# Output products one step later, two element-wise sets interleaved on VectorE, all output copies on ScalarE

## Chip, cores, metric

One core of one Trainium2 chip. The metric is the device time of one execution in microseconds, here 1134.75 us as the median of three runs (1134.71 to 1135.37).

## What is computed

The reference is a linear attention followed by a two-layer network. For each of 8 batches and 8 heads (576 tokens, head size 64), queries and keys go through a feature map of 128 features, `exp` of plus and minus the projection less its largest magnitude. Sums over keys give `kv` and `z`, and each query's output is a quotient. The heads are put together to x, 4608 tokens by 512, and then

```python
h = x @ w_in            # 512 -> 2048
g = h - np.tanh(h)
return (g @ w_out)      # 2048 -> 512
```

## The kernel before

**First part** (up to some 329 us): attention, 32 units of two heads; x goes transposed to DRAM (`xs`). Meanwhile the weights of the network are decoded into f32 tiles (`dec_*`), and some are split. Each unsplit weight tile has a home (`HOME`, `w_home`): a `tl` slot of a lasting pool, or a pool that is closed when group 1 begins. `second` closes that pool and opens another, `rp`, with the weight sums `th`, and with slots `tp` and `xs`.

**Second part** (from line 552): the network. Tokens are cut into 9 groups of 512 (four tiles of 128). The hidden width of 2048 is cut into 16 blocks f of 128, and a step handles one group g and one pair of blocks j (f = 2j and 2j+1): 72 steps s, group by group. Each f32 operand is kept as a high part in fp32r and a low remainder, and each product is made of three matmuls, high with high, high with low, low with high.

In groups 0 and 1 (steps 0 to 15) a step is *plain*: `plain` makes 12 matmuls of 512 columns for each block (4 chunks of the contraction, 3 each), into one PSUM tile for each block. The tiles alternate between the pairs y, x and w, v. From group 2 on (`FOLD`, steps 16 to 71) a step is *folded*: seven products of quarter size (`product`, six matmuls of 256 columns each, 42 in all) of sums and differences of weight and token quarters, and VectorE adds them up to the same two blocks, in Y (first token half) and X (second token half). W holds products 1 and 6, V 5 and 7, Y 2 and 3, X's first half 4. The adds are u3 (line 884), K (885), the Y add (891) and the two X adds (892, 893). K's first part is a ScalarE copy of product 1.

Each step gives two *sets* (`Set`): in a plain step one for each block with all four token tiles, in a folded step one for tiles 0 and 1 and one for tiles 2 and 3, with both blocks. A set is a 128x512 piece of h on which `h - tanh(h)` is made with care near zero. Its instructions are, by name: `y_` (square, ScalarE), `s1_`, `s2_` (squares with an offset, ScalarE), `th_` (tanh), `mk_` (mask of large values, ScalarE), `d1`, `d2`, `d3` (polynomial, VectorE, lines 610, 613, 616), `d4` (h minus tanh, 619), `d5` (select by the mask, 622), `gh_` (high part, ScalarE, 626), `gl_` (low part, GpSimd, 630). The tiles `y`, `s1`, `th` and `mk` have one buffer for both sets, `s2`, `gh` and `gl` two. `d1`, `d2`, `d5` read two SBUF tiles; `d3`, `d4` and the five adds read PSUM.

`q` multiplies a set's high and low parts by the output weights `wo[g, f]` into one PSUM tile per token tile (four buffers): for one token tile and a folded set six matmuls of 512 columns. After the last pair of blocks of a group the four tiles are copied out of PSUM (`finish`) and stored by DMA. `wo_fetch` loads a step's two output weights (512 KB each) on SP's queue into four buffers in turn.

All instructions of the second part are issued in an order written out by hand, the loop over s at the end of the function. Each engine takes its own in that order. `one` and `two` are the last step's two sets. Other work is hung into the loop by `job(s, place, ...)` and comes out at `do(s, place)`: weight splits of group 0 (`LOWS`), loads, the weight sums for the folded products (`t_load`/`t_new`, `t_add`, `t_hi`, `t_lo`; one j a step), the last four units' denominators (`den_mul`, `x_store`), and each next group's token operands: for group 1 plain ones, from group 2 on seven sums and differences (`x_sum` on GpSimd, `x_hi` on ScalarE, `x_lo` on GpSimd). Their places are the slots of `x_slot`. GpSimd's jobs at place `p1` stand behind a tiny copy (`mark`, line 903) that reads a VectorE result.

Of the kernel before, what the change touches and what calls it, by code (L numbers as in the profile page):

```python
# [19 lines left out]
P = 128  # L20
# [12 lines left out]
def tile_linear_attention_moe(  # L33
# [57 lines left out]
    HOME = {("i", f): f for f in range(NI, NF)} | {("o", f): f - NO for f in range(NO, NO + NI)}  # L91
# [42 lines left out]
    slots = [*range(12), 0, 1, 2, 3, 4, 5, 6, 7, 12]  # L134

    def x_slot(nm):
        k = slots.pop(0)
        if not slots:
            slots.extend((8, 9, 10, 11, 0, 1, 2, 3, 4, 5, 6, 7, 12))
        return (tp[0] if k == 12 else xp[k // 4]).tile([P, 2, DM], F32R, tag="tp" if k == 12 else f"xc{k}", name=f"xc{nm}")  # L140

    with ExitStack() as c1:
# [301 lines left out]
        def period(i):  # L444
# [42 lines left out]
            if last:  # L487
                for j in range(NCT):
                    x0.append(x_slot(f"0_{j}"))
                    nc.scalar.copy(x0[j][:, 0, :], xt[0][:, j, :])  # L490
                    nc.vector.tensor_tensor(x0[j][:, 1, :], xt[0][:, j, :], f32(x0[j][:, 0, :]), ALU.subtract)
# [60 lines left out]
    with ExitStack() as c2, tc.manual_schedule():  # L552
# [12 lines left out]
        def second():  # L565
            late.close()
            pool = c2.enter_context(tc.tile_pool(name="rp", bufs=1, reuse_waits="tile", side="right"))
            th.extend(pool.tile([P, DM], F32R, name=f"th{j}") for j in range(NP))
            tp.append(pool)
            xp.append(pool)  # L570
# [8 lines left out]
        class Set:  # L579
            def __init__(self, s, half, h, fs, tiles):  # L580
                self.g, self.j = steps[s]
                self.s, self.h, self.fs, self.tiles = s, h, fs, tiles
                self.nm = f"{s}_{half}"
                self.left = list(tiles)
# [52 lines left out]
        ends = []  # L637
        mark = gp.tile([P, 1], F32, name="gate")

        def q(v, most=4):  # L640
            if v is None:
                return
            g = v.g
            for t in v.left[:most]:
                v.left.remove(t)
                if (g, t) not in po:
                    po[g, t] = [ps_o.tile([P, DM], F32, tag="o", name=f"po{g}_{t}"), False]
                o, begun = po[g, t]
                n = v.tiles.index(t)
                cuts = [slice((a * len(v.tiles) + n) * P, (a * len(v.tiles) + n + 1) * P) for a in range(len(v.fs))]  # L650
                last = v.fs[-1] == NF - 1
                for f, cut in zip(v.fs, cuts):
                    for k in range(2):
                        nc.tensor.matmul(o, v.gh[:, cut], wo[g, f][:, k, :], start=not begun, stop=False)  # L654
                        begun = True
                for f, cut in zip(v.fs, cuts):
                    nc.tensor.matmul(o, v.gl[:, cut], wo[g, f][:, 0, :], start=False, stop=last and f == v.fs[-1])  # L657
                po[g, t][1] = True
                if last:
                    ends.append((g, t))  # L660

        def finish(g, t):
            pool, tag = (gp, "o") if t < 2 else (tp[0], "xs")
            o = pool.tile([P, DM], F32, tag=tag, name=f"o{g}_{t}", bufs=2)
            if t % 2:
                nc.scalar.copy(o, po[g, t][0])
            else:
                nc.vector.tensor_copy(o, po[g, t][0])
            nc.sync.dma_start(out[(g * GT + t) * P : (g * GT + t + 1) * P, :], o)
# [55 lines left out]
        def t_new(j):  # L725
            pool, tag = (xp[0], "xc3") if j % 2 and j < NP - 1 else (tp[0], "tp")
# [34 lines left out]

        xsum = {}
# [8 lines left out]
        def x_new(g, n):  # L771
            xc.setdefault(g, {})[n] = x_slot(f"{g}_{n}")
# [28 lines left out]
        def job(s, where, fn, *args):  # L801
            jobs.setdefault((s, where), []).append((fn, args))
# [6 lines left out]
        LOWS = ["i8 i9 o8", "i10 i11 o9", "o4 o5 i12", "o6 o7", "i13 o10 o11", "i14 i15 o12", "o13 o14 o15"]  # L809
# [7 lines left out]
        for j, s in enumerate((9, 10, 11, 12, 13, 14, 15, 19)):  # L817
            job(s - 1, "d1", t_load if 2 * j < NI else t_new, j)
            job(s, "d1", t_add, j)
            job(s, "a1", t_hi, j)  # L820
            job(s + 1, "v0", t_lo, j)
# [3 lines left out]
        for k, s in enumerate((0, 1, 2, 3)):  # L825
            job(s, "p1", den_mul, units[NU - 4 + k], nc.gpsimd)
            job(s, "p1", x_store, units[NU - 4 + k])
        for g in range(1, NG):
            z = NP * (g - 1)

            def fresh(c, g=g):
                if c == 0:
                    xr[g] = x_raw(g)
                x_load(g, xr[g], slice(c, c + 2))

            job(z, "d1", fresh, 0)
            job(z + 1, "d", fresh, 2)
            if g < FOLD:
                for c, n in enumerate((4, 5, 6, 7) if g == 1 else (2, 3, 5, 6)):
                    job(z + n, "a", x_plain, g, c)  # L840
                    job(z + n, "p1", x_plain_lo, g, c)
                continue
            for n, where, fn, k in (
                (1, "a", x_hi, 1), (1, "p1", x_lo, 1),
                (2, "p0", x_sum, 5), (2, "a", x_hi, 2), (2, "p1", x_lo, 2),
                (3, "p0", x_sum, 6), (3, "a", x_hi, 5), (3, "p1", x_lo, 5),
                (4, "p0", x_sum, 3), (4, "a", x_hi, 6), (4, "p1", x_lo, 6),
                (5, "p0", x_sum, 7), (5, "a", x_hi, 3), (5, "p1", x_lo, 3),
                (6, "a", x_hi, 7), (6, "p1", x_lo, 7),
                (7, "a", x_hi, 4), (7, "p1", x_lo, 4),  # L850
            ):
                job(z + n, where, fn, g, k)

        for s in range(NS + 1):
            one, two = sets.get((s - 1, 0)), sets.get((s - 1, 1))
            g, j = steps[s] if s < NS else (None, None)
            do(s, "d")
            fold = g is not None and g >= FOLD
            if g is not None:
                Y, X = (ps_x.tile([P, GN], F32, tag=t, name=f"y{s}" if a == 0 else f"x{s}") for a, t in enumerate("yx" if fold or s % 2 else "wv"))  # L860
                if g:
                    wo_fetch(g, j)
            if fold:
                W, V = (ps_x.tile([P, GN], F32, tag=t, name=f"{t}{s}") for t in "wv")
                r = {1: W[:, lo_], 6: W[:, hi_], 2: Y[:, lo_], 3: Y[:, hi_], 4: X[:, lo_], 5: V[:, lo_], 7: V[:, hi_]}
                K = gp.tile([P, 3, HN], F32, tag="k", name=f"k{s}")
                for n in (1, 6, 5, 7):
# [4 lines left out]
            if g is not None:  # L872
                cur = [Set(s, a, h, (2 * j, 2 * j + 1) if fold else (2 * j + a,), (2 * a, 2 * a + 1) if fold else (0, 1, 2, 3)) for a, h in enumerate((Y, X))]
            run(two, "d3", "d4", "d5")
            do(s, "v0")
            do(s, "d1")
            run(two, "gh_")
            run(one, "gl_")
            run(two, "gl_")
            do(s, "p0")  # L880
            if fold:
                u3 = K[:, 2, :]
                both = u3.unsqueeze(1).broadcast_to([P, 2, HN])
                tt(u3, r[6], K[:, 0, :], ALU.add)
                tt(K[:, 1:3, :], V.rearrange("p (a n) -> p a n", a=2), both, ALU.add)  # L885
                for n in (3, 2):
                    product(r[n], g, j, n)
                if s < NS - 1:
                    q(one, 1)
                product(X[:, lo_], g, j, 4)  # L890
# [3 lines left out]
            elif g is not None:  # L894
                plain(X, g, 2 * j + 1)
            q(one)
            q(two)
            do(s, "a")
            if g is not None:
                new, nxt = cur  # L900
                run(new, "y_", "s1_", "s2_", "th_", "mk_", "d1", "d2")
                if (s, "p1") in jobs:
                    nc.gpsimd.tensor_copy(mark, new.s1[:, 0:1])
                do(s, "p1")
                run(new, "d3", "d4", "d5")
                run(nxt, "y_", "s1_", "s2_")
                run(new, "gh_")
                do(s, "v1")
                run(nxt, "th_", "mk_", "d1", "d2")
            do(s, "p2")  # L910
            do(s, "v")
            do(s, "a1")
            while ends:
                finish(*ends.pop(0))
            if g is not None:
                sets[s, 0], sets[s, 1] = cur
# [55 lines left out]
```

## Time and profile before

| | |
|---|---|
| median of three runs | 1134.75 us |
| profiled execution: time, span | 1136.19 us, 1134.4 us |
| granted TensorE clock, mean | 0.998 |
| busy TensorE, VectorE, ScalarE, GpSimd | 98%, 85%, 76%, 46% |
| first matmul of step 0, first of step 16 | 328.84 us, 501.38 us |

The span runs from the first to the last instruction; the profiled execution's time has 1.79 us around it. In the rows of a timeline the first figure is the start, the second the duration, both in us from the span's start; then engine, line, operation, what is written and read, how many; in brackets the idle time before it and what ended it. PE is TensorE, PEld its weight loads, DVE VectorE, ACT ScalarE, POOL GpSimd, SP the queue of the DMAs. In the rows by stretch the columns are the stretch, its length, busy us and count for PE, PEld, DVE, ACT and POOL, then granted clock, busy share of the DMA engines, GB/s. A row of one line of code gives count, then shortest, median and longest duration in ns.

### The profile page before, as it was taken

To read this page: it belongs to the slowest core of one execution; us is meant where nothing else is said; L and a number is where in the kernel's file an instruction comes from. 1 tells how busy PE (TensorE), PEld (TensorE's weight loads), DVE (VectorE), ACT (ScalarE), POOL (GpSimd) and SP (SyncE) were. 2 spreads that over 40 slices of the span, in tenths; PEclk is the share of its full clock that TensorE was granted. 3 is DMA by queue.
4 is the path that set the end of the run, shared out by engine and by line. 5 is a ranking of instruction groups with operands and counts; after the bars stand their busy time and mean duration, and the time that the engine had idled before them with its cause. 6 is when DMAs were issued, how large, how long until landed. Compare 5 with 4: busy or idle time off the path is not lost. (4 is left out here: it accounts for less than half of the span.)

```text
span 1134.4 us, 22407 instructions
## 1 busy us (share of the span) xinstructions
PE 1113.2 (98%) x8010; PEld 894.6 (79%) x8010; DVE 964.5 (85%) x1478; ACT 860.4 (76%) x1716; POOL 525.5 (46%) x508
## 2 busy tenths in 40 slices
PE   9999999999999999999899999999999999999997
PEld 6666666666667888888788888888888888888885
DVE  6888889888879879998888888888888888888886
ACT  5888888888888877677677777777777776877765
POOL 4665665565534434443443543543543543443231
PEclk9999999999999999999999999999999999999999
DMA  5576766667624246324225325234333323422432
GB/s 162 181 242 220 237 216 211 237 219 246 204 92 153 97 155 198 112 93 151 92 82 179 106 81 185 77 111 152 108 113 127 133 96 115 161 76 95 136 105 75
DMA packets 76048, 165.41 MB, mean 146 GB/s; under 512 B 16672, under 2 KB 31392, under 8 KB 75936
## 3 DMA queue, kind: packets, MB, share of 16 engines
q1 hardware_dynamic: 75776, 163.90, 43.2%
q8 instruction: 64, 1.05, 0.4%
q14 instruction: 48, 0.39, 0.1%
q10 hardware_dynamic: 160, 0.07, 0.0%
HBM read 134.28 MB, written 29.51 MB: 144 GB/s over the span
## 5 line engine op out<-in xcount | busy, mean ns | idle before, releaser
L630 POOL TENSOR_TENSOR gl<-s,gh 128x512 fp32r<-128x512 f32 x143 | 216.9, 1517 | 325.2 <-ACT gh L626 188.5
L654 PE MATMUL po<-wo,gh 128*128 128x512 f32 x1152 | 326.8, 396 | 5.5 <-ACT mk L607 3.4
L654 PEld LDWEIGHTS po<-wo,gh 128*128 128x128 f32 x1152 | 209.3, 189 | 49.1 <-ACT mk L607 4.6
L657 PE MATMUL po<-wo,gl 128*128 128x512 f32 x576 | 197.7, 406 | 5.4 <-POOL gl L630 5.1
L626 ACT CAST gh<-s 128x512 fp32r<-128x512 f32 x144 | 89.5, 621 | 109.1 <-DVE s L622 99.1
L657 PEld LDWEIGHTS po<-wo,gl 128*128 128x128 f32 x576 | 104.8, 189 | 47.7 <-POOL gl L630 26.0
L610 DVE SCALAR_TENSOR_TENSOR s<-s,y 128x512 f32<-128x512 f32 x144 | 99.4, 690 | 47.8 <-ACT s L595 47.8
L255 DVE TENSOR_REDUCE m<-pp 128x4 f32<-128x512 f32 (+3 forms) x98 | 92.0, 940 | 40.9 <-PE pp L245 37.4
L314 POOL TENSOR_TENSOR ss<-ss,kp 128x512 f32<-128x512 f32 x96 | 122.9, 1280 | 8.0 <-ACT kp L299 3.0
L622 DVE COPY_PREDICATED s<-mk,th 128x512 f32<-128x512 uint32 x144 | 111.1, 771 | 15.2 <-ACT s L595 0.5
L595 ACT ACTIVATE s<-y,bias_t 128x512 f32<-128x512 f32 x144 | 104.3, 724 | 20.0 <-DVE s L616 11.1
L299 ACT ACTIVATE kp<-t 128x256 f32<-128x256 f32 (+2 forms) x256 | 108.8, 484 | 7.8 <-DVE t L262 7.0
L613 DVE SCALAR_TENSOR_TENSOR s<-s,s 128x512 f32<-128x512 f32 x144 | 99.7, 693 | 15.0
L607 ACT ACTIVATE mk<-y,bias_t 128x512 f32<-128x512 f32 x144 | 102.6, 712 | 0.0
L599 ACT ACTIVATE s<-y,bias_t 128x512 f32<-128x512 f32 x144 | 102.1, 709 | 0.0
L245 PEld LDWEIGHTS pp<-wph,qk 64*128 64x128 f32 x1152 | 72.1, 187 | 33.3 <-PE po L350 13.1
L262 DVE TENSOR_TENSOR t<-pp,m 128x512 f32<-128x512 f32 (+3 forms) x98 | 92.0, 941 | 3.3
L245 PE MATMUL pp<-wph,qk 64*128 64x128 f32 x1152 | 90.3, 289 | 1.2 <-PE pk L319 0.8
L591 ACT ACTIVATE y<-y 128x512 f32<-128x512 f32 x72 | 43.0, 597 | 63.9 <-DVE y L891 57.8
L713 PE MATMUL y<-xc,hl 128*128 128x256 f32 x672 | 89.3, 282 | 1.7 <-DVE th L619 1.7
L713 PEld LDWEIGHTS y<-xc,hl 128*128 128x128 f32 x672 | 84.1, 189 | 2.0 <-issue 1.6
L713 PEld LDWEIGHTS w<-xc,hl 128*128 128x128 f32 x560 | 78.0, 188 | 5.1
(396 smaller groups left out, 2242.7 us busy)
## 6 DMA issues: line engine op xcount, KB each, us to landing
wo<-wod SPq DMA_DIRECT2D x128, 512.0 KB
qk<-in_qkT SPq DMA_DIRECT2D x31, 576.0 KB
v<-in_v SPq DMA_DIRECT2D x32, 320.0 KB
rb<-rr SPq DMA_DIRECT2D x64, 144.0 KB
xs<-rb SPq DMA_DIRECT2D x32, 288.0 KB
out<-o SPq DMA_DIRECT2D x36, 256.0 KB
rawi<-in_moe_w_in SPq DMA_DIRECT2D x16, 512.0 KB
rawo<-in_moe_w_out SPq DMA_DIRECT2D x16, 512.0 KB
```

Source lines behind the costliest of these rows:

```text
L245: nc.tensor.matmul(heads[e][:, o * F : (o + 1) * F], u.qk[hs, j * P : (j + 1) * P], wph[hs, :], start=True, stop=True)
L299: nc.scalar.activation(o, x, AF.Exp, scale=1.0 - 2.0 * s)
L314: nc.gpsimd.tensor_tensor(u.ss, u.ss, u.kp[:, :, j], ALU.add)
L595: nc.scalar.activation(self.s1, self.y, AF.Square, bias=bias_t[:, 0:1])
L599: nc.scalar.activation(self.gs, self.y, AF.Square, bias=bias_t[:, 1:2])
L607: nc.scalar.activation(self.mk, self.y, AF.Relu, bias=bias_t[:, 2:3])
L613: stt(self.s1, self.gs, PC2, self.s1, ALU.add, ALU.mult)
L622: nc.vector.copy_predicated(self.gs, self.mk.bitcast(U32), self.th)
L630: (nc.vector if self.s == NS - 1 and self.tiles[0] else nc.gpsimd).tensor_tensor(self.gl, self.gs, f32(self.gh), ALU.subtract)
L654: nc.tensor.matmul(o, v.gh[:, cut], wo[g, f][:, k, :], start=not begun, stop=False)
L657: nc.tensor.matmul(o, v.gl[:, cut], wo[g, f][:, 0, :], start=False, stop=last and f == v.fs[-1])
L713: nc.tensor.matmul(o, w[:, k], x[:, a, m], start=(i == 0), stop=(i == 5))
```

## The change

- Outputs a step later. The loop knows a third set, `old`, the second set of two steps ago. A step's output products are now `q(old)` in the middle of the step's hidden products and `q(one)` behind them; `q(two)` in the same step is gone. Folded: products 1, 6, 5, 7; `q(old)`; 3, 2, 4; `q(one)`. In a folded set, `q` runs the high matmuls of both tiles first and then the low ones. The loop has one more turn at its end.
- VectorE's order in a folded step: `d3`, `d4` of `two`; the five adds; `d5` of `two`; then `d1` to `d5` of the new first set, `d1`, `d2` of the second. `mk_` of a folded second set moves to the next step on ScalarE, and `gh_`, `gl_` of `two` come behind the new set's squares.
- All four output copies of a group go to ScalarE; the tiles lie in token slots instead of own ones.
- The weight sums move to steps 8 to 15 (before: 9 to 15, and j = 7 in step 19). The homes of unsplit output weights change (`HOME`), so that o8 to o15 outlast the closed pool, and the split of o15 moves to step 7.
- The last units' denominators go to steps 1 to 4 instead of 0 to 3, group 1's token operands one step earlier with their low parts where they were. From group 3 on all GpSimd token work is at place `p0`, ahead of the low parts, with no `mark`.

```diff
-        def q(v, most=4):
+        def q(v):
...
+            if nt == 2:
+                for part in (high, low):
+                    for n in range(nt):
+                        part(n)
             else:
-                nc.vector.tensor_copy(o, po[g, t][0])
+                for n in range(nt):
+                    high(n)
+                    low(n)
+
+        def finish(n):
+            while ends and ends[0][1] < n:
+                store(*ends.pop(0))
+
+        def store(g, t):
+            if t % 2 == 0:
+                out_t[g, t // 2] = x_slot(g + 2, f"o{g}_{t}", 2 + t // 2, F32)
+            o = out_t[g, t // 2][:, t % 2, :]
+            nc.scalar.copy(o, po[g, t])
...
-        for j, s in enumerate((9, 10, 11, 12, 13, 14, 15, 19)):
-            job(s - 1, "d1", t_load if 2 * j < NI else t_new, j)
-            job(s, "d1", t_add, j)
+        for j in range(NP):
+            s = NP + j
+            job(s - 1 if j else s, "d1" if j else "d", t_load if 2 * j < NI else t_new, j)
+            job(s, "d1" if j else "v", t_add, j)
...
-        for s in range(NS + 1):
-            one, two = sets.get((s - 1, 0)), sets.get((s - 1, 1))
+        for s in range(NS + 2):
+            one, two, old = sets.get((s - 1, 0)), sets.get((s - 1, 1)), sets.get((s - 2, 1))
...
-            run(two, "d3", "d4", "d5")
+            q(old)
+            finish(2)
+            do(s, "a")
+            if not plain_two:
+                run(two, "mk_")
+            finish(4)
+            run(two, "d3", "d4")
+            if not fold:
+                run(two, "d5")
             do(s, "v0")
             do(s, "d1")
-            run(two, "gh_")
-            run(one, "gl_")
-            run(two, "gl_")
             do(s, "p0")
             if fold:
-                u3 = K[:, 2, :]
-                both = u3.unsqueeze(1).broadcast_to([P, 2, HN])
                 tt(u3, r[6], K[:, 0, :], ALU.add)
-                tt(K[:, 1:3, :], V.rearrange("p (a n) -> p a n", a=2), both, ALU.add)
-                for n in (3, 2):
+                tt(K[:, 1:3, :], V.rearrange("p (a n) -> p a n", a=2), u3.unsqueeze(1).broadcast_to([P, 2, HN]), ALU.add)
+                for n in (3, 2, 4):
                     product(r[n], g, j, n)
-                if s < NS - 1:
-                    q(one, 1)
-                product(X[:, lo_], g, j, 4)
+            elif g is not None:
+                plain(X, g, 2 * j + 1)
+            q(one)
+            if fold:
                 tt(Y, Y, K[:, 0:2, :].rearrange("p a n -> p (a n)"), ALU.add)
                 tt(X[:, hi_], r[5], u3, ALU.add)
                 tt(r[4], r[4], u3, ALU.add)
-            elif g is not None:
-                plain(X, g, 2 * j + 1)
-            q(one)
-            q(two)
-            do(s, "a")
+                run(two, "d5")
             if g is not None:
-                new, nxt = cur
-                run(new, "y_", "s1_", "s2_", "th_", "mk_", "d1", "d2")
+                run(new, "y_", "s1_", "s2_")
+            run(two, "gh_", "gl_")
+            if g is not None:
+                run(new, "th_", "mk_", "d1", "d2")
...
                 run(new, "d3", "d4", "d5")
+                do(s, "v1")
                 run(nxt, "y_", "s1_", "s2_")
-                run(new, "gh_")
-                do(s, "v1")
-                run(nxt, "th_", "mk_", "d1", "d2")
-            do(s, "p2")
+                run(new, "gh_", "gl_")
+                run(nxt, "th_", "d1", "d2")
+                if not fold:
+                    run(nxt, "mk_")
```

More of the change, by code (lines that the diff above doesn't have):

```diff
@@ L90, in tile_linear_attention_moe @@
     wd = {f: dram.tile([P, DM], F32, name=f"wdi{f}") for f in range(NI)}
-    HOME = {("i", f): f for f in range(NI, NF)} | {("o", f): f - NO for f in range(NO, NO + NI)}
+    HOME = {("i", f): f for f in range(NI, NF)} | {("o", f): f - NI for f in range(NI, NF)}
     def w_home(nm, f):
@@ L132, in x_load, with x_slot @@
             o += n
[L134 to L140, printed above, removed]
+    def x_slot(g, nm, n, dt=F32R):
+        k = (4 * g + n) if g < 2 else (8, 9, 10, 11, 0, 1, 2, 4, 5, 6, 7, 3, 12, 13)[g % 2 * 7 + n]
+        return (tp[k - 12] if k > 11 else xp[k // 4]).tile([P, 2, DM], dt, tag="tp" if k > 11 else f"xc{k}", name=f"xc{nm}")
     with ExitStack() as c1:
@@ L488, in period @@
                 for j in range(NCT):
-                    x0.append(x_slot(f"0_{j}"))
+                    x0.append(x_slot(0, f"0_{j}", j))
                     nc.scalar.copy(x0[j][:, 0, :], xt[0][:, j, :])
@@ L568, in second @@
             th.extend(pool.tile([P, DM], F32R, name=f"th{j}") for j in range(NP))
-            tp.append(pool)
+            tp.extend((pool, gp))
             xp.append(pool)
@@ L583, in __init__ @@
                 self.nm = f"{s}_{half}"
-                self.left = list(tiles)
             def tile(self, tag, dt=F32, bufs=1):
@@ L635, in run, with cuts, high @@
                     getattr(what, n)()
-        ends = []
-        mark = gp.tile([P, 1], F32, name="gate")
-        def q(v, most=4):
+        ends, out_t = [], {}
+        def q(v):
             if v is None:
                 return
[L643 to L652, printed above, removed]
+            g, nt = v.g, len(v.tiles)
+            last = v.fs[-1] == NF - 1
+            def cuts(n):
+                return [(f, slice((a * nt + n) * P, (a * nt + n + 1) * P)) for a, f in enumerate(v.fs)]
+            def high(n):
+                t = v.tiles[n]
+                begun = (g, t) in po
+                if not begun:
+                    po[g, t] = ps_o.tile([P, DM], F32, tag="o", name=f"po{g}_{t}")
+                for f, cut in cuts(n):
@@ L653, in q, with low @@
                     for k in range(2):
-                        nc.tensor.matmul(o, v.gh[:, cut], wo[g, f][:, k, :], start=not begun, stop=False)
+                        nc.tensor.matmul(po[g, t], v.gh[:, cut], wo[g, f][:, k, :], start=not begun, stop=False)
                         begun = True
-                for f, cut in zip(v.fs, cuts):
-                    nc.tensor.matmul(o, v.gl[:, cut], wo[g, f][:, 0, :], start=False, stop=last and f == v.fs[-1])
-                po[g, t][1] = True
+            def low(n):
+                t = v.tiles[n]
+                for f, cut in cuts(n):
+                    nc.tensor.matmul(po[g, t], v.gl[:, cut], wo[g, f][:, 0, :], start=False, stop=last and f == v.fs[-1])
@@ L659, in q @@
                 if last:
                     ends.append((g, t))
[L662 to L666, printed above, removed]
-            else:
-                nc.vector.tensor_copy(o, po[g, t][0])
+            if nt == 2:
+                for part in (high, low):
+                    for n in range(nt):
+                        part(n)
+            else:
+                for n in range(nt):
+                    high(n)
+                    low(n)
@@ L725, in t_new @@
         def t_new(j):
-            pool, tag = (xp[0], "xc3") if j % 2 and j < NP - 1 else (tp[0], "tp")
+            pool, tag = (xp[0], "xc3") if j % 2 else (tp[0], "tp")
             t = pool.tile([P, 2, DM], F32, tag=tag, name=f"tp{j}")
@@ L760, in raw @@
             return xr[g][:, 2 * c : 2 * c + 2, r * HN : (r + 1) * HN]
+        mark = gp.tile([P, 1], F32, name="gate")
         xsum = {}
@@ L771, in x_new @@
         def x_new(g, n):
-            xc.setdefault(g, {})[n] = x_slot(f"{g}_{n}")
+            x = xc.setdefault(g, {})
+            x[n] = x_slot(g, f"{g}_{n}", len(x))
         def x_sum(g, n):
@@ L808, in tile_linear_attention_moe @@
         job(NP, "d", second)
-        LOWS = ["i8 i9 o8", "i10 i11 o9", "o4 o5 i12", "o6 o7", "i13 o10 o11", "i14 i15 o12", "o13 o14 o15"]
+        LOWS = ["i8 i9 o8", "i10 i11 o9", "o4 o5 i12", "o6 o7", "i13 o10 o11", "i14 i15 o12", "o13 o14", "o15"]
         for k, ts in enumerate(LOWS):
@@ L824, in tile_linear_attention_moe @@
             job(k, "v", den_spread, units[NU - 3 + k])
-        for k, s in enumerate((0, 1, 2, 3)):
+        for k, s in enumerate((1, 2, 3, 4)):
             job(s, "p1", den_mul, units[NU - 4 + k], nc.gpsimd)
@@ L838, in tile_linear_attention_moe @@
             if g < FOLD:
-                for c, n in enumerate((4, 5, 6, 7) if g == 1 else (2, 3, 5, 6)):
+                for c, n in enumerate((3, 4, 5, 6)):
                     job(z + n, "a", x_plain, g, c)
-                    job(z + n, "p1", x_plain_lo, g, c)
+                    job(z + n + 1, "p1", x_plain_lo, g, c)
                 continue
-            for n, where, fn, k in (
+            FIRST = (
                 (1, "a", x_hi, 1), (1, "p1", x_lo, 1),
@@ L846, in tile_linear_attention_moe @@
                 (3, "p0", x_sum, 6), (3, "a", x_hi, 5), (3, "p1", x_lo, 5),
[L847 to L851, printed above, removed]
+                (4, "p0", x_sum, 3), (4, "a", x_hi, 6), (4, "a", x_hi, 4), (4, "p1", x_lo, 6),
+                (5, "a", x_hi, 3), (5, "p1", x_lo, 4),
+                (6, "p0", x_sum, 7), (6, "p1", x_lo, 3),
+                (7, "a", x_hi, 7), (7, "p1", x_lo, 7),
+            )
+            NEXT = (
+                (2, "a", x_hi, 1), (2, "a", x_hi, 2), (2, "p0", x_sum, 5),
+                (3, "a", x_hi, 5), (3, "a", x_hi, 4), (3, "p0", x_sum, 6), (3, "p0", x_lo, 1),
+                (4, "a", x_hi, 6), (4, "p0", x_lo, 5), (4, "p0", x_sum, 3),
+                (5, "a", x_hi, 3), (5, "p0", x_lo, 6), (5, "p0", x_sum, 7),
+                (6, "a", x_hi, 7), (6, "p0", x_lo, 3), (6, "p0", x_lo, 2),
+                (7, "p0", x_lo, 7), (7, "p0", x_lo, 4),
+            )
+            for n, where, fn, k in FIRST if g == FOLD else NEXT:
                 job(z + n, where, fn, g, k)
-        for s in range(NS + 1):
-            one, two = sets.get((s - 1, 0)), sets.get((s - 1, 1))
+        for s in range(NS + 2):
+            one, two, old = sets.get((s - 1, 0)), sets.get((s - 1, 1)), sets.get((s - 2, 1))
             g, j = steps[s] if s < NS else (None, None)
+            fold = g is not None and g >= FOLD
+            plain_two = two is not None and steps[s - 1][0] < FOLD
             do(s, "d")
-            fold = g is not None and g >= FOLD
             if g is not None:
@@ L862, in tile_linear_attention_moe @@
                     wo_fetch(g, j)
+                new, nxt = (Set(s, a, h, (2 * j, 2 * j + 1) if fold else (2 * j + a,), (2 * a, 2 * a + 1) if fold else (0, 1, 2, 3)) for a, h in enumerate((Y, X)))
+                sets[s, 0], sets[s, 1] = new, nxt
             if fold:
@@ L866, in tile_linear_attention_moe @@
                 K = gp.tile([P, 3, HN], F32, tag="k", name=f"k{s}")
+                u3 = K[:, 2, :]
                 for n in (1, 6, 5, 7):
@@ L871, in tile_linear_attention_moe @@
                 plain(Y, g, 2 * j)
-            if g is not None:
-                cur = [Set(s, a, h, (2 * j, 2 * j + 1) if fold else (2 * j + a,), (2 * a, 2 * a + 1) if fold else (0, 1, 2, 3)) for a, h in enumerate((Y, X))]
-            run(two, "d3", "d4", "d5")
+            q(old)
[7 more added lines that the diff above has]
+                run(two, "d5")
             do(s, "v0")
             do(s, "d1")
-            run(two, "gh_")
-            run(one, "gl_")
-            run(two, "gl_")
             do(s, "p0")
             if fold:
-                u3 = K[:, 2, :]
-                both = u3.unsqueeze(1).broadcast_to([P, 2, HN])
                 tt(u3, r[6], K[:, 0, :], ALU.add)
-                tt(K[:, 1:3, :], V.rearrange("p (a n) -> p a n", a=2), both, ALU.add)
-                for n in (3, 2):
+                tt(K[:, 1:3, :], V.rearrange("p (a n) -> p a n", a=2), u3.unsqueeze(1).broadcast_to([P, 2, HN]), ALU.add)
+                for n in (3, 2, 4):
                     product(r[n], g, j, n)
-                if s < NS - 1:
-                    q(one, 1)
-                product(X[:, lo_], g, j, 4)
+            elif g is not None:
+                plain(X, g, 2 * j + 1)
+            q(one)
+            if fold:
                 tt(Y, Y, K[:, 0:2, :].rearrange("p a n -> p (a n)"), ALU.add)
@@ L893, in tile_linear_attention_moe @@
                 tt(r[4], r[4], u3, ALU.add)
-            elif g is not None:
-                plain(X, g, 2 * j + 1)
-            q(one)
-            q(two)
-            do(s, "a")
+                run(two, "d5")
             if g is not None:
-                new, nxt = cur
-                run(new, "y_", "s1_", "s2_", "th_", "mk_", "d1", "d2")
+                run(new, "y_", "s1_", "s2_")
+            run(two, "gh_", "gl_")
+            if g is not None:
+                run(new, "th_", "mk_", "d1", "d2")
                 if (s, "p1") in jobs:
                     nc.gpsimd.tensor_copy(mark, new.s1[:, 0:1])
-                do(s, "p1")
+                    do(s, "p1")
                 run(new, "d3", "d4", "d5")
+                do(s, "v1")
                 run(nxt, "y_", "s1_", "s2_")
-                run(new, "gh_")
-                do(s, "v1")
-                run(nxt, "th_", "mk_", "d1", "d2")
-            do(s, "p2")
+                run(new, "gh_", "gl_")
+                run(nxt, "th_", "d1", "d2")
+                if not fold:
+                    run(nxt, "mk_")
             do(s, "v")
             do(s, "a1")
[L913 to L916, printed above, removed]
+        finish(4)
 def _bits(u):
```

## The prediction

> **What bounds the kernel now.** I read the page's first lines, then the table of stretches, then TensorE's timeline, and last VectorE's and GpSimd's timelines inside one step of the second part.
>
> ```profile
> span 1134.4 us, 22407 instructions
> PE 1113.2 (98%) x8010; PEld 894.6 (79%) x8010; DVE 964.5 (85%) x1478; ACT 860.4 (76%) x1716; POOL 525.5 (46%) x508
> 400.00:450.00 50.00, 50.00 (x219) 40.84 (x218) 42.25 (x61) 37.37 (x64) 19.98 (x17) 1.00 0.56 189
> 950.00:1000.00 50.00, 49.32 (x298) 42.66 (x297) 42.62 (x71) 37.40 (x65) 21.72 (x20) 1.00 0.34 117
> 1100.00:1134.40 34.40, 26.72 (x134) 21.51 (x133) 23.63 (x38) 18.67 (x32) 7.58 (x5) 0.95 0.23 79
> ```
>
> TensorE looks full, at a granted clock of 1.00, but its records overlap (a matmul's record is longer than the distance to the next), so small waits vanish in "98%". What it lost has to be counted from starts.
>
> ```profile
> 328.84 3.01 PE L722 MATMUL y<-xc,hl 128*128 128x512 f32 x12
> 331.69 2.88 PE L722 MATMUL x<-xc,hl 128*128 128x512 f32 x12
> 334.41 2.88 PE L722 MATMUL y<-xc,hl 128*128 128x512 f32 x12
> 501.38 1.11 PE L713 MATMUL w<-xc,hl 128*128 128x256 f32 x8
> 559.80 1.11 PE L713 MATMUL w<-xc,hl 128*128 128x256 f32 x8
> 768.73 1.11 PE L713 MATMUL w<-xc,hl 128*128 128x256 f32 x8
> 856.42 1.11 PE L713 MATMUL w<-xc,hl 128*128 128x256 f32 x8
> 988.21 1.10 PE L713 MATMUL w<-xc,hl 128*128 128x256 f32 x8
> 993.52 0.30 PEld L657 LDWEIGHTS po<-wo,gl 128*128 128x128 f32 x2 [0.39 <-POOL gl L630]
> 997.59 1.10 PE L654 MATMUL po<-wo,gh 128*128 128x512 f32 x4
> 998.99 1.10 PE L713 MATMUL w<-xc,hl 128*128 128x256 f32 x8
> 1108.03 1.11 PE L713 MATMUL w<-xc,hl 128*128 128x256 f32 x8
> 1129.99 0.63 PE L657 MATMUL po<-wo,gl 128*128 128x512 f32 x2
> 999.15 1.41 PE w L713 x12
> 1000.56 1.41 PE v L713 x12
> 1001.98 1.43 PE y L713 x12
> 1003.41 0.92 PE po L654 x4
> ```
>
> (The last four rows are of the chain that ended last.) Work without waits: twelve plain matmuls 334.41 - 331.69 = 2.72; six output matmuls of one token tile 998.99 - 997.59 = 1.40; 36 products of a folded step 1003.41 - 999.15 = 4.26, so all 42 take 4.97. The second part holds 32 plain blocks (87.0), 72 steps with four tiles each (72 x 5.60 = 403.2) and 56 folded steps (56 x 4.97 = 278.3): 768.5 us. It runs from 328.84 to 1129.99 + 0.63 less the 0.17 by which a record overhangs its slot, 1130.45: 801.6 us. **Lost: 33.1 us.** Where: up to the first folded step 172.5 for 171.0 of work, 1.5. Steps 16 to 20 (501.38 to 559.80) 58.4 for 5 x 10.57, 5.6. Steps 21 to 70 (to 1108.03) 548.2 for 528.5, 19.7: a quiet step takes 998.99 - 988.21 = 10.78, 0.21 too much, ended by GpSimd's low part (the PEld row), and a group of eight 87.69 instead of 84.56, so some 1.4 more where groups change. From the last step's start 22.4 for 16.2, 6.25.
>
> **Why it waits.** In a folded step the outputs consume both sets of the step just before, so the chain adds, squares, polynomial, select, high, low must end in time for the same step's output matmuls. VectorE is the slow member:
>
> ```profile
> 987.16 0.69 DVE L610 SCALAR_TENSOR_TENSOR s<-s,y 128x512 f32<-128x512 f32 x1 [0.69 <-ACT s L595]
> 990.17 0.78 DVE L622 COPY_PREDICATED s<-mk,th 128x512 f32<-128x512 uint32 x1
> 990.83 0.68 DVE L610 SCALAR_TENSOR_TENSOR s<-s,y 128x512 f32<-128x512 f32 x1
> 991.62 0.69 DVE L613 SCALAR_TENSOR_TENSOR s<-s,s 128x512 f32<-128x512 f32 x1
> 995.76 0.70 DVE L891 TENSOR_TENSOR y<-y,k 128x512 f32<-128x512 f32 x1
> 996.36 0.42 DVE L892 TENSOR_TENSOR x<-v,k 128x256 f32<-128x256 f32 x1
> 996.82 0.43 DVE L893 TENSOR_TENSOR x<-x,k 128x256 f32<-128x256 f32 x1
> 997.94 0.69 DVE L610 SCALAR_TENSOR_TENSOR s<-s,y 128x512 f32<-128x512 f32 x1 [0.69 <-ACT s L595]
> 996.55 0.60 ACT L591 ACTIVATE y<-y 128x512 f32<-128x512 f32 x1 [0.81 <-DVE y L891]
> 997.18 0.72 ACT L595 ACTIVATE s<-y,bias_t 128x512 f32<-128x512 f32 x1
> 991.79 1.67 POOL L630 TENSOR_TENSOR gl<-s,gh 128x512 fp32r<-128x512 f32 x1 [1.56 <-ACT gh L626]
> 995.35 1.30 POOL L630 TENSOR_TENSOR gl<-s,gh 128x512 fp32r<-128x512 f32 x1 [1.88 <-issue]
> L741 DVE TENSOR_TENSOR tp<-tp x16: 419/426/1562, 425.7 to 465.6; 128x256 f32<-128x256 f32 x16
> ```
>
> Its period (997.94 - 987.16 = 10.78) is 10.09 of work and one wait of 0.69: after the adds it has nothing to do until ScalarE has made the first square.
>
> **The change, part by part.**
>
> *Order in a folded step.* TensorE: 24 products (2.84), outputs of the second set of two steps ago (2.80, to 5.64), 18 products (to 7.77), outputs of the first set of the last step (to 10.57). Instructions are the same; only order and deadlines move. VectorE does the select of the older set between the adds and the new polynomial. Count from its Y add as 0: X adds at 0.60 and 1.06, the old select at 1.52, free at 2.18 (a select takes 990.83 - 990.17 = 0.66 of the queue). The square is done 997.18 + 0.72 - 995.76 = 2.14 after that add. So the 0.69 wait is filled almost exactly, and the period falls to about 10.1. I add 0.1 because the second set's square follows four or five ScalarE instructions and is as close; 10.2. The Y products end at 7.06 in the step, so the Y add starts near 7.25 and recurs every 10.57: VectorE then has 0.4 to spare, and **TensorE sets the step at 10.57.**
>
> *Deadlines.* With ScalarE's instructions 0.63 apart (997.18 - 996.55) the older set's high part ends about 3.3 after the Y add, the new set's about 7.1; that is 10.6 in this step and 3.8 in the next. In the next step they are wanted at 2.84 and at 7.77: 2.8 and 4.0 of slack, and a low part of 1.3 to 1.7 on GpSimd fits, wanted another 1.9 later. PSUM: W and V are read until 8.4 in the step, rewritten at 10.57; X is freed by the difference of line 619 at about 5.4 and written at 7.1. Nothing is late next but VectorE, by 0.4.
>
> *ScalarE* copies all four output tiles of a group instead of two, and a mask moves into the next step. It is busy 37.40 of 50, 8.1 of 10.78; two copies more (0.58 each by the row below) in eight steps add 0.15 a step: 8.2 of 10.57. Four copies in one step, 2.3, end before its next square is due with about 0.4 left. VectorE is rid of two copies. The next group's first output bank is free at about 5.2 and wanted at 7.77, so the group change should cost nothing. Cost 0; without that cover the old 1.4 for each of seven groups, 9.8.
>
> *Weights.* A step's output weights stay a step longer in four buffers, so SP's fetch waits to 5.64 in the step and has 12.5 us until 7.77 in the next. Queued behind it on SP are loads of raw x (needed two steps on) and stores of outputs. The transfers:
>
> ```profile
> 901.00:905.00 4.00, 4.00 (x35) 4.00 (x34) 3.56 (x7) 3.73 (x7) 2.29 (x3) 1.00 0.78 262
> 905.00:912.00 7.00, 7.00 (x37) 5.63 (x36) 5.73 (x11) 4.56 (x9) 3.52 (x5) 1.00 0.01 2
> 1122.34 1.19 PE L654 MATMUL po<-wo,gh 128*128 128x512 f32 x4 [2.14 <-ACT gh L626]
> 1124.14 1.14 PE L657 MATMUL po<-wo,gl 128*128 128x512 f32 x2 [0.61 <-POOL gl L630]
> 1130.65 0.58 ACT L666 COPY o<-po 128x512 f32<-128x512 f32 x1 [2.21 <-PE po L657]
> ```
>
> A step's megabyte passes in 4 us and then the queue is dark. Cost 0; if one pair took over 12.5, the excess each step.
>
> *Weight sums* move one step up, the last from step 19 to 15, into plain steps. Each is four subtractions (0.43, up to 1.56 when GpSimd is running), two low parts, two ScalarE copies; for the first four also two SP loads, the first of them now at the top of step 8. In the plain steps a set's outputs gain about 9 us of slack, so VectorE may fall behind there unseen; at step 16 I find it up to 2 late against 2.1 of slack in W and V. The 5.6 of steps 16 to 20 goes; I keep 1.0 (between 0 and 4). The moved split of o15, the denominators a step later and x of group 1 a step earlier lie under the same slack: 0.
>
> *Start.* Step 1 no longer runs both sets: its wait goes, part of the 1.5.
>
> *End.* The last Y add comes at 7.25 in the last step, the new set's high part at 14.4, while TensorE has output work to 13.4: 1.1 lost. The last set's high part comes 10.5 after the Y add, 17.8, work ends at 17.3: 0.6 lost. Sum 1.7 instead of 6.25; last matmul to end of span unchanged.
>
> The last stretch's mean clock, 0.95 of 34.4 us, is 1.7 us of clock lost, and the two waits of 2.14 and 0.61 within 4 us are the only large ones there. I take full clock at the new end; if it drops again, 1.7 more. The Trainium skill, TensorE: Matmul & The Clock Gate, section Why this matters for your kernels, asks for gaps of about 3 us before the clock drops: by that rule the new end keeps the clock as well, though the trace shows it dropped after less.
>
> **Sum.** Span 1134.4 - 33.1 + 1.7 + 1.0 = 1104.0. The profiled execution took 1136.19 (1.79 around its span) and would take 1105.8; it stands 1.44 above the median of the runs shown, 1134.75, so the median becomes 1104.4.
>
> **Rivals.** *VectorE keeps its wait* (0.10): if the square comes later than 2.18, the select only shifts the wait and the step stays at 10.78. Then 56 x 0.21 = 11.8 is not won: 1116. For it: the two numbers meet within 0.04. Against: 0.4 of spare per step.
>
> *GpSimd gets in VectorE's way in part* (0.13). The row of 995.35 has the low part at 1.30 and that of 991.79 at 1.67, where it began beside a VectorE instruction with two SBUF inputs (991.62); and the subtractions spread from 0.43 to 1.56. In the new order the older low part fits between the polynomial's second instruction (ends 3.66) and the select (5.19): 1.3 in 1.53. Each 0.2 that VectorE is pushed past 10.57 costs 56 x 0.2 = 11: 1115.
>
> *Slower: that collision in every step* (0.06). The low part starts late by more than 0.24, and the select waits for nearly all of it: 1.29 less 0.47 spare is 0.82 a step, 1104.4 + 45.9 = 1150. It decides from (1134.75 - 1104.4)/56 + 0.47 = 1.01 us blocked per step. Against: the Y add re-aligns VectorE to TensorE each step, so a slip doesn't grow. The Trainium skill, SBUF — State Buffer, section SBUF: two separate sides, says that GpSimd and a two-input VectorE instruction take the shared ports whole, the later one blocking; the rows of 1.67 and 1.56 agree, and by that rule alone the collision lasts the whole low part.
>
> *No net change* (0.05): the waits come back at group changes and in steps 16 to 20, some 1125 to 1136.
>
> **How the numbers follow.** The forecast has 0.66, own range 1101 to 1108 (down to 1101 if the end loses nothing and the slots are 1 us shorter in sum). Up to 1118 the first rival and most of the second are in. Faster 0.66 + 0.10 + 0.13 + 0.02, same 0.02, slower 0.06 + 0.01. 0.2% (2.3 us) is about what this kernel's runs can tell.
>
> **What would show it.** Steps at 10.5 to 10.6 between w rows; no "gl" row on PEld in quiet steps; the 0.69 wait of L610 gone and a wait at the Y add in its place; group length near 84.6. Wrong if the Y add no longer waits for TensorE: then VectorE is the bound; or if fetches gate the outputs.

## The result, and the profile after

The changed kernel took 1108.17 us as a median of four runs, against 1135.06: a ratio of 0.977 (95% interval 0.975 to 0.979). In a later run, beside two variants, it took 1107.52 (one of its five executions there took 2767.7 us and stands outside every ratio). Faster, as forecast; the forecast was 1104.4, its range 1101 to 1118. The result lies 3.8 above the forecast, and 0.2 above the 1101 to 1108 that the prediction gives for the forecast without its rivals.

The first lines of the changed kernel's page, then two rows of its table of stretches (columns as before):

```profile
span 1106.9 us, 22300 instructions
PE 1097.0 (99%) x8010; PEld 897.6 (81%) x8010; DVE 954.8 (86%) x1460; ACT 856.9 (77%) x1734; POOL 515.8 (47%) x465
500.00:550.00 50.00, 48.33 (x290) 43.04 (x291) 43.54 (x72) 38.43 (x69) 20.03 (x16) 0.97 0.36 119
950.00:1000.00 50.00, 50.00 (x317) 45.03 (x316) 43.09 (x72) 37.68 (x67) 24.95 (x19) 1.00 0.31 106
```

In the late stretch TensorE now runs 50.00 of 50 with 317 matmuls where it ran 298; VectorE and ScalarE have about as much to do in it as before. One folded step of the changed kernel, from its timeline:

```profile
966.10 1.12 PE L722 MATMUL w<-xc,hl 128*128 128x256 f32 x8
976.68 1.12 PE L722 MATMUL w<-xc,hl 128*128 128x256 f32 x8
971.30 1.31 POOL L800 TENSOR_TENSOR xc<-xsum,xc 128x512 fp32r<-128x512 f32 x1
972.04 0.69 DVE L911 TENSOR_TENSOR k<-v,k 128x512 f32<-128x512 f32 x1
973.37 0.70 DVE L918 TENSOR_TENSOR y<-y,k 128x512 f32<-128x512 f32 x1 [0.64 <-PE y L722]
974.90 0.75 DVE L617 COPY_PREDICATED s<-mk,th 128x512 f32<-128x512 uint32 x1
975.56 0.69 DVE L605 SCALAR_TENSOR_TENSOR s<-s,y 128x512 f32<-128x512 f32 x1
976.04 0.61 ACT L621 CAST gh<-s 128x512 fp32r<-128x512 f32 x1
976.72 1.48 POOL L625 TENSOR_TENSOR gl<-s,gh 128x512 fp32r<-128x512 f32 x1 [2.75 <-ACT gh L621]
978.62 0.78 DVE L617 COPY_PREDICATED s<-mk,th 128x512 f32<-128x512 uint32 x1
```

The step takes 976.68 - 966.10 = 10.58 (10.78 before). The old select (974.90) sits where VectorE used to wait for ScalarE's square: the first polynomial instruction follows at once, 2.19 after the Y add. In place of that wait stands one of 0.64 at the Y add, for TensorE: TensorE sets the step. No weight load waits for a low part any more, and the older set's low part (976.72 to 978.20) ends before the next select of VectorE (978.62).

Counted from starts as in the prediction: the first row below opens step 0, the next three steps 16, 21 and 71, and the last ends the matmuls.

```profile
328.70 3.01 PE L731 MATMUL y<-xc,hl 128*128 128x512 f32 x12
497.34 1.11 PE L722 MATMUL w<-xc,hl 128*128 128x256 f32 x8
553.86 1.11 PE L722 MATMUL w<-xc,hl 128*128 128x256 f32 x8
1082.32 1.10 PE L722 MATMUL w<-xc,hl 128*128 128x256 f32 x8
1101.96 1.10 PE L656 MATMUL po<-wo,gl 128*128 128x512 f32 x4
```

Up to step 16 it takes 168.6 for 168.2 of work (2.8 of output work has moved behind that point), steps 16 to 20 take 56.5 for 52.85, steps 21 to 70 take 528.5 for 528.5, and from there 20.6 for 19.0 (the same 2.8 more). Lost: 0.4, 3.7, 0 and 1.6, in sum 5.7 of the 33.1 before.

What is still lost, from the same timeline: one wait in the first folded step (step 16), and two at the end.

```profile
497.19 1.54 POOL L625 TENSOR_TENSOR gl<-s,gh 128x512 fp32r<-128x512 f32 x1 [3.35 <-issue]
497.49 1.78 DVE L605 SCALAR_TENSOR_TENSOR s<-s,y 128x512 f32<-128x512 f32 x1
500.20 0.18 POOL L928 COPY gate<-s 128x1 f32<-128x1 f32 x1 [1.48 <-DVE s L608]
500.34 1.28 POOL L800 TENSOR_TENSOR xc<-xsum,xc 128x512 fp32r<-128x512 f32 x1
501.67 0.38 PE L722 MATMUL v<-xc,hl 128*128 128x256 f32 x1 [1.93 <-POOL xc L800]
1096.51 2.13 PE L650 MATMUL po<-wo,gh 128*128 128x512 f32 x8 [0.55 <-ACT gh L621]
1099.99 2.13 PE L650 MATMUL po<-wo,gh 128*128 128x512 f32 x8 [0.41 <-ACT gh L621]
```

Read the first five rows downwards: GpSimd's low part begins 0.3 before VectorE's two-input instruction, which then takes 1.78 instead of 0.69; the gate waits for VectorE, token operand 7's low part for the gate, and TensorE's product 7 for that, 1.93. In this execution the clock was halved behind that wait (0.97 in the stretch from 500), which makes the other 1.7 of the 3.7.

### The profile page after: what moved, and what is told of

The parts are those of the page before. It is cut to its first block, busy times and chain, and to the rows that moved or that the text cites. A ratio compares the mean times of both kernels' runs of the same rounds, so it can differ in the third digit from the quotient of the medians.

```text
span 1106.9 us, 22300 instructions
## 1 busy us (share of the span) xinstructions
PE 1097.0 (99%) x8010; PEld 897.6 (81%) x8010; DVE 954.8 (86%) x1460; ACT 856.9 (77%) x1734; POOL 515.8 (47%) x465
## 4 chain that ended last, share of the span: by engine, by line
PE 89%; DVE 6%; ACT 2%; issue 1%; DMA 0%; SPq 0%; DVEq 0%; ACTq 0%; POOL 0%; POOLq 0%
PE po L650 21%; PE po L656 10%; PE pp L241 7%; PE y L722 7%; PE v L722 7%; PE w L722 7%; PE pc L301 7%; PE po L346 6%; PE x L722 4%; PE pd L361 3%; PE ptt L268 3%; PE y L731 2%; PE x L731 2%; DVE tp L750 1%; DVE s L617 1%; DVE s L605 1%
## 5 line engine op out<-in xcount | busy, mean ns | idle before, releaser
L650 PE MATMUL po<-wo,gh 128*128 128x512 f32 x1152 | 308.8, 396 | 1.0 <-ACT gh L621 1.0
L656 PE MATMUL po<-wo,gl 128*128 128x512 f32 x576 | 173.9, 397 | 0.0
L656 PEld LDWEIGHTS po<-wo,gl 128*128 128x128 f32 x576 | 108.5, 188 | 26.2
L617 DVE COPY_PREDICATED s<-mk,th 128x512 f32<-128x512 uint32 x144 | 116.2, 807 | 9.1
L608 DVE SCALAR_TENSOR_TENSOR s<-s,s 128x512 f32<-128x512 f32 x144 | 106.5, 740 | 16.1 <-ACT gh L621 1.4
L605 DVE SCALAR_TENSOR_TENSOR s<-s,y 128x512 f32<-128x512 f32 x144 | 101.9, 708 | 3.3 <-ACT s L590 3.2
L722 PEld LDWEIGHTS y<-xc,hl 128*128 128x128 f32 x672 | 87.1, 188 | 5.1
```

What stands on the lines that cost most here:

```text
L605: stt(self.s1, self.s1, PC1, self.y, ALU.add, ALU.mult)
L608: stt(self.s1, self.gs, PC2, self.s1, ALU.add, ALU.mult)
L617: nc.vector.copy_predicated(self.gs, self.mk.bitcast(U32), self.th)
L650: nc.tensor.matmul(po[g, t], v.gh[:, cut], wo[g, f][:, k, :], start=not begun, stop=False)
L656: nc.tensor.matmul(po[g, t], v.gl[:, cut], wo[g, f][:, 0, :], start=False, stop=last and f == v.fs[-1])
L722: nc.tensor.matmul(o, w[:, k], x[:, a, m], start=(i == 0), stop=(i == 5))
```

## Experiments

Each is the changed kernel with one edit, the last with two. Ratios are to the kernel before, 95% intervals behind them.

**The wait of step 16, first try** (`e1_x7_ahead`).

```diff
-                (7, "a", x_hi, 7), (7, "p1", x_lo, 7),
+                (7, "a", x_hi, 7), (7, "p0", x_lo, 7),
```

> Theory: the changed kernel's missing 4 us lie at step 16. There TensorE waits 1.93 us for the low part of token operand 7, which GpSimd may start only behind the gate (a VectorE result that came late), and the clock is then halved for 3.4 us. With that low part put ahead of the gate the wait goes and with it the halved clock: 1104 to 1105 us, granted clock 1.00 in that stretch. Rival: GpSimd's low part only changes places with something that is as late (VectorE held off by GpSimd), and the time stays at 1107 to 1109.

1107.92 us, 0.976 (0.974 to 0.977): the rival was right. Its timeline has the same loss under another name:

```profile
506.56 0.51 PE L722 MATMUL x<-xc,th 128*128 128x256 f32 x2 [1.73 <-DVE th L614]
```

Now TensorE waits 1.73 for VectorE to free X. The wait for GpSimd was a sign of VectorE being late. In this run's profile the clock stayed whole.

**Depth without the interleave** (`e2_select_first`).

```diff
-            if not fold:
-                run(two, "d5")
+            run(two, "d5")
...
                 tt(r[4], r[4], u3, ALU.add)
-                run(two, "d5")
```

> The old select put back in front of the adds in the folded steps, everything else as changed. Theory: VectorE has its 0.69 us wait for ScalarE's square again, its period is 10.78 and becomes the bound of the folded steps: 56 x 0.2 more, 1118 to 1121 us. Rival, that the later products alone bring the gain: 1107 to 1110.

1156.73 us, 1.019 (1.017 to 1.020): slower than the kernel before. The direction was forecast, the size was not: 49 us and not 10 to 13. A step of it, from its timeline:

```profile
911.76 1.11 PE L722 MATMUL w<-xc,hl 128*128 128x256 f32 x8
913.05 0.69 DVE L605 SCALAR_TENSOR_TENSOR s<-s,y 128x512 f32<-128x512 f32 x1 [0.68 <-ACT s L590]
919.36 1.29 POOL L800 TENSOR_TENSOR xc<-xsum,xc 128x512 fp32r<-128x512 f32 x1
919.72 0.50 PE L722 MATMUL x<-xc,th 128*128 128x256 f32 x2 [0.75 <-DVE th L614]
919.77 1.51 DVE L617 COPY_PREDICATED s<-mk,th 128x512 f32<-128x512 uint32 x1
923.33 1.10 PE L722 MATMUL w<-xc,hl 128*128 128x256 f32 x8
```

The step takes 11.57, as most do. VectorE's wait is back (0.68). Beside it the select takes 1.51 instead of 0.76, because it stands where GpSimd's token work (919.36) now runs. VectorE is the bound and frees X late (0.75). The two causes can be told apart: in the last group, where GpSimd has no token work, the selects take 0.75 to 0.78 and steps 67 to 70 take 10.85 to 10.88. That is the price of the wait alone, near the 10.78 that was reckoned, and it leaves nothing of the gain (10.81 to 10.83 in the same steps before the change). The rest is GpSimd and, in 18 steps, a wait of the select for the mask (9.1 us in all), which the change had moved a step later.

**Interleave without the depth** (`e3_same_step`).

```diff
-            q(old)
             finish(2)
...
             run(two, "gh_", "gl_")
+            q(two)
```

> Output products of both last sets in the same step again (order first set, second set, behind all hidden products), VectorE's new order kept. If the filled wait on VectorE is what counts: the older set's high part comes at 7.8 in the step, wanted at 7.77, the low part at 9.4, wanted at 9.6, so the folded steps stay within 0.1 of 10.58; the plain steps and steps 16 to 20 have less slack: 1109 to 1114 us. Rival, that depth carries it: TensorE waits for GpSimd's low part in every folded step, 0.2 us or more each, 1119 or above.

1120.52 us, 0.987 (0.985 to 0.988): the time that the rival named (1119 or above), but not for its reason. Two rows of its timeline, a step apart:

```profile
968.85 1.11 PE L722 MATMUL w<-xc,hl 128*128 128x256 f32 x8
979.55 0.63 PE L722 MATMUL w<-xc,hl 128*128 128x256 f32 x4
```

The step takes 10.70. Its list of waits (waiter, releaser; us in all, count, longest) says for what:

```profile
PEld po L650 <- ACT gh L621: 21.8, 59, 2.2
PEld po L656 <- POOL gl L625: 5.4, 8, 1.2
```

The high part, wanted in the same step, comes a little late in nearly every one (59 waits). The low part, which the rival named, is waited for only 8 times. Steps 21 to 70 take 536.1 in this execution instead of 528.5, which is 7.7 of the 12 us that separate it from the whole change. Of the rest, 3.1 lie ahead of step 16 and 1.3 in steps 16 to 20; that the shorter chain has less slack there for a late VectorE is likely, but I did not follow it.

**Output copies on VectorE** (`e4_dve_copies`).

```diff
-            nc.scalar.copy(o, po[g, t])
+            (nc.scalar.copy if t % 2 else nc.vector.tensor_copy)(o, po[g, t])
```

> Output copies of tiles 0 and 2 on VectorE as before the change. Theory: the copy of tile 2 can't start before 5.5 in the step and stands ahead of the differences that free X, wanted at 7.1; some 0.4 to 1.0 us of waiting at each of eight group changes: 1111 to 1116 us. Rival, that the copies don't matter since VectorE has 0.8 us to spare in a step: 1107 to 1109.

1113.93 us, 0.981 (0.980 to 0.982). As expected, and the copies lie where expected:

```profile
597.80 1.12 PE L722 MATMUL w<-xc,hl 128*128 128x256 f32 x8
603.18 0.69 DVE L677 COPY xco<-po 128x512 f32<-128x512 f32 x1 [0.71 <-PE po L656]
604.38 0.68 DVE L614 TENSOR_TENSOR th<-x,th 128x512 f32<-128x512 f32 x1
608.72 1.11 PE L722 MATMUL w<-xc,hl 128*128 128x256 f32 x8
```

VectorE waits 0.71 for the tile and frees X only behind the copy; the step takes 10.92 instead of 10.58. Seven such steps are 2.4 us. The rest of the 6 lies in the plain steps (1.7), in a longer wait at step 16 (2.97 instead of 1.90 to 1.93), and in the clock: three of its four executions show 0.996 to 0.998, the profiled one does not.

**Last weight sum in step 19** (`e5_sum7_late`), and **in step 16** (`e7_sum7_at16`).

```diff
-            s = NP + j
+            s = NP + j if j < NP - 1 else 19      # e5
+            s = NP + j if j < NP - 1 else 16      # e7
```

(In the first its tile lies in the slot `tp`, as before the change.)

> The last weight sum back in step 19 (load 18, low parts 20), in the folded steps, as before the change. If slack from the deeper order is what removed the 5.6 us of steps 16 to 20: step 15 is relieved, the folded steps take the sum out of 0.8 us of spare each and 2.1 us of slack, 1104 to 1107 us. If the move into plain steps removed them: the waits of 1 us and more on VectorE's differences come back at steps 19 to 21 and the time is 1109 or above.

> The last weight sum (j = 7) made in step 16 instead of 15, its low parts in step 17. Theory: what is late at step 16 is VectorE itself, loaded in step 15 with the sum's four subtractions and held off by GpSimd; whichever of its products TensorE needs first becomes the wait (token operand 7's low part as changed, the freeing of X in the run with that low part ahead). Without these 2 to 3 us in step 15 both waits go and the clock stays whole: 1104 to 1105.5 us. Rival: the lateness comes from step 9 (ScalarE's wait on group 0's outputs) or is only moved into step 16: a wait of 1 us or more remains near 500 to 515 and the time is 1107 to 1109.

Step 19: 1110.35 us, 0.978 (0.976 to 0.979), as the second theory had it. Step 16: 1106.20 us, 0.974 (0.973 to 0.976), between the two forecasts. First a row of the timeline with the sum in step 16:

```profile
500.59 0.38 PE L722 MATMUL v<-xc,hl 128*128 128x256 f32 x1 [0.25 <-POOL xc L800]
```

Then four of the timeline with the sum in step 19:

```profile
536.74 1.48 POOL L800 TENSOR_TENSOR xc<-xr,xc 128x512 fp32r<-128x512 f32 x1
537.00 1.51 DVE L750 TENSOR_TENSOR tp<-wi 128x256 f32<-128x256 f32 x1
549.39 0.50 PE L722 MATMUL x<-xc,th 128*128 128x256 f32 x2 [1.06 <-DVE th L614]
562.64 0.50 PE L722 MATMUL x<-xc,th 128*128 128x256 f32 x2 [1.07 <-DVE th L614]
```

Relieving step 15 shrinks the wait of step 16 from 1.93 to 0.25: VectorE's load there was its cause. In step 19 the sum costs 4 us more than in step 16, mainly as waits for X in two steps. Both steps are folded. But in step 19 the subtractions meet GpSimd's token work and stretch (1.51 in the row, 0.42 in step 16, where none runs beside them). So it is the place that sets the price, and moving the sum out of step 19 is a part of the gain of its own, some 2 to 3 us.

**GpSimd's token work behind the low part** (`e6_pool_behind`): the `p0` entries of NEXT come out behind `run(two, "gh_", "gl_")`.

> GpSimd's token work of groups 3 to 8 put behind the older set's low part instead of ahead of it, so that it runs while VectorE has its select and polynomial instructions with two SBUF inputs. Same work. If GpSimd and such an instruction exclude each other: steps with two pieces of token work (five in eight) lose 1 us or more beyond VectorE's spare, 1125 to 1145 us, and selects or first polynomial instructions of 1.5 us and more in the trace. If they only share: 1107 to 1110.

1171.01 us, 1.032 (1.030 to 1.034): exclusion, and more of it than I had reckoned. Its timeline:

```profile
962.16 1.29 POOL L800 TENSOR_TENSOR xc<-xsum,xc 128x512 fp32r<-128x512 f32 x1
962.62 1.46 DVE L617 COPY_PREDICATED s<-mk,th 128x512 f32<-128x512 uint32 x1
963.42 1.78 POOL L800 TENSOR_TENSOR xc<-xr,xc 128x512 fp32r<-128x512 f32 x1
963.98 1.77 DVE L605 SCALAR_TENSOR_TENSOR s<-s,y 128x512 f32<-128x512 f32 x1
968.93 0.50 PE L722 MATMUL x<-xc,th 128*128 128x256 f32 x2 [1.91 <-DVE th L614]
```

The records overlap, but the work does not: the four end at 963.45, 964.08, 965.20 and 965.75, each behind the one before by a little less than it takes alone (0.77, 1.29, 0.69 for the last three). TensorE waits 1.91 for X. The rule of the Trainium skill, SBUF — State Buffer, section SBUF: two separate sides (the shared ports are held for a whole instruction, the later one blocks), agrees with these rows: 0.77 became 1.46, 0.69 became 1.77. Not all of the loss is the collision: the granted clock was 0.99, which is some 12 of the 63 us.

**More work for VectorE** (`e8_dve_more`): the add u3 made three times.

> The add u3 made three times in each folded step instead of once (same result), about 1.0 us more for VectorE, just ahead of its wait for the Y products. If TensorE sets the step and VectorE has the 0.64 us of that wait to spare, about 0.36 us a step is over: 1124 to 1130 us. If VectorE were the bound already, 56 us more: 1160 or above. If its slack were larger than 1.0: 1108.

1134.38 us, 0.999 (0.998 to 1.000): more than expected, far less than if VectorE had been the bound already. From its timeline:

```profile
950.34 1.10 PE L722 MATMUL w<-xc,hl 128*128 128x256 f32 x8
961.30 1.10 PE L722 MATMUL w<-xc,hl 128*128 128x256 f32 x8
...
946.61 1.33 DVE L911 TENSOR_TENSOR k<-w,k 128x256 f32<-128x256 f32 x3
948.84 0.70 DVE L919 TENSOR_TENSOR y<-y,k 128x512 f32<-128x512 f32 x1
```

The wait at the Y add is gone, and the step has grown to 10.96. Two adds of 0.46 (1.33 less 0.41) cost 0.38 of 0.92, so about 0.54 a step was free, 0.1 less than the wait suggested. Ten steps take 11.3: with VectorE as the bound, a pause of 0.4 shows in it every 59 us, for which the profile names no cause.

**The last three side by side** (`after_again`, `e7_again`, and `e9_both`: the sum in step 16 and token operand 7 a place earlier).

> The changed kernel once more, to stand beside the next two on the same chip: 1107 to 1109 us, a run that falls into the halved clock near 503 us up to 1111.

> The last weight sum in step 16, a second time: 1105.5 to 1106.5 us if the 2 us it won are its own, 1107 or above if they came from the chip.

> The last weight sum in step 16, and token operand 7 of group 2 a place earlier, its low part ahead of the gate. If the 0.41 us that TensorE still waits there is all that is left at step 16: 1105.0 to 1106.0 us. If GpSimd then holds off VectorE instead: no gain, 1106 or above.

1107.52, 1106.14 and 1106.93 us; 0.9752 (0.974 to 0.977), 0.9742 (0.973 to 0.976), 0.9750 (0.974 to 0.976). The sum in step 16 was the fastest both times, by 1.4 us here, with intervals that overlap: faster than the kernel before for certain, faster than the change by about as much as its runs can tell. Moving operand 7 as well takes back half of it.

## Why the prediction was right

*Lost time counted from starts.* The 33.1 us of TensorE's waits were the right stock to count: of the span's 27.5 us won, all came out of it (5.7 are left), TensorE's own work being the same.

*The folded step.* 10.57 forecast, 10.58 measured, and 528.5 for steps 21 to 70, as forecast; 0.4 of spare forecast for VectorE, 0.54 measured by the added work. The claim that the select fills the wait is shown from both sides, by the changed kernel's rows and by the run that puts it back.

*Depth and interleave.* I took them together, and rightly, but not for the whole reason. Without the depth the rest of the change still gives 14.5 us (1120.52); without the interleave it gives none (1156.73). My price for a VectorE that keeps its wait, 1116, assumed that all else stays. It holds about where GpSimd has no token work (10.86 a step, 10.78 reckoned). Elsewhere that work had been placed for the new order, and out of it the collision costs more than the wait.

*GpSimd in VectorE's way.* The collision behind the rival of 1150 is real: forced with the token work it gave 1171, some 12 of it clock. The one that the rival spoke of, the low part against the select, did not come, by 0.42 (978.20 to 978.62); no run forced it. The token work escapes by place: it runs while VectorE reads PSUM (971.30 beside 972.04, which keeps its 0.69).

*Output copies, weights.* Group changes cost nothing, as forecast: a group of eight takes 84.62 (585.53 to 670.15), 84.56 forecast. Without cover I had 1.4 for each of seven changes, 9.8; with the copies back on VectorE each costs 0.35, 2.4 in sum, and the rest of that run's 6 us comes from elsewhere. No fetch of weights gated an output.

*End.* 1.7 forecast; 0.55 and 0.41 in the rows, and 1.6 counted by starts; eight matmuls behind a wait also take longer, 2.13 (1096.51) instead of 2.02 (1090.08). The clock stayed whole there, as forecast.

*Where it was off by 3.8.* The term that was mis-sized is the 1.0 kept for steps 16 to 20: they lost 3.7. The wait there was 1.93. I had VectorE "up to 2 late against 2.1 of slack" in W and V, but the first to suffer was token operand 7 behind its gate, and X, which have less. Behind that wait the clock was halved in some executions, 1.7 more; I had looked for this at the end only. (Two of the four executions kept a whole clock: 1107.33 and 1107.61.) With the sum in step 16 the same steps lose 0.6. Another 0.9 is the 1.44 that I took off because the profiled execution stood so far above the median: the new one, 1108.73, stands only 0.56 above its median.

## What to carry to other kernels

When an engine's records overlap, count its lost time from the starts of its instructions and compare with the bare work; "98% busy" hid 33 us. To close a wait of one engine for another inside a loop, look for an independent instruction of just that length from a neighbouring set, and give the consumer a step of slack; either alone may do little or harm, because the rest of the schedule was laid out for both. A wait's releaser names who came last, not who is to blame: relieve it, and see whether the wait goes or only changes its name.

## What the runs showed of the hardware that I had not expected

The halved clock did not follow the length of the wait. At step 16 the clock was halved behind a wait of 1.93 in one execution of the changed kernel, and stayed whole behind 1.90 in another, and behind 2.97 in the run with copies on VectorE. The thirteen traces show what decides: in each, the clock changes only at times that lie whole multiples of 3.413 us apart. Here are stretches cut at such times, two of the changed kernel's first trace, then two of its second:

```profile
499.36:502.77 3.41, 1.48 (x11) 1.23 (x10) 3.15 (x5) 2.25 (x4) 1.42 (x2) 1.00 0.25 100
502.77:506.19 3.42, 3.42 (x9) 2.69 (x9) 3.21 (x6) 2.71 (x6) 1.68 (x1) 0.50 0.00 0
498.55:501.96 3.41, 1.89 (x17) 1.69 (x15) 3.17 (x4) 1.15 (x3) 1.93 (x3) 1.00 0.46 154
501.96:505.38 3.42, 3.04 (x16) 2.60 (x17) 3.11 (x6) 3.31 (x7) 1.84 (x2) 1.00 0.00 0
```

In the first trace the whole wait falls into one stretch (3.41 less 1.48 is 1.93 idle), and the next one has half the clock. In the second the wait lies across a cut, 1.52 on one side and 0.38 on the other, and the clock stays whole. Over all thirteen traces, ten such stretches ahead of the last matmul have 1.90 us or more without a matmul record, and the clock is halved in the stretch behind each of them; behind the others, which have at most 1.80, it never is. So a wait of 2 us costs 1.7 more or nothing, by luck of where it falls. No run varied the idle time on purpose, and the ends of matmul records are modelled, so the bound between 1.80 and 1.90 is what these traces show and no more. The Trainium skill, TensorE: Matmul & The Clock Gate, section What's actually happening, describes a free-running window of about 3.4 us over which activity is judged; the traces agree, with 3.413.
